# First attention layer of a four-layer network on one core: the order of statistics, norms and transposes between the value and key products of its prologue

## The chip, the core and the metric

The kernel runs on one core of one Trainium2 chip. A core has five engines that run side by side and wait for one another through semaphores: PE (TensorE, matrix products and transposes; its weight loads are listed as PEld), DVE (VectorE, elementwise work and row statistics), ACT (ScalarE, copies with a function), POOL (GpSimd) and SP (SyncE, which here issues the DMAs). Each engine works off its own instructions in the order in which the program lists them. What counts is the device time of one execution in microseconds (us), the median of several runs.

## The reference

Four layers on x of 2048 rows and 640 columns: attention, Fourier mixing, attention, Fourier mixing, each with a layer norm ahead of it and a residual sum behind it.

```python
def _A_ref(x, wqkv, wo):                     # attention, 32 heads of 20, window 256
    qkv = (x @ wqkv).reshape(B, S, 3, H, Dh) ...
    scores = einsum("bhqd,bhkd->bhqk", q, k) * Dh ** -0.5
    p = softmax(where(mask, scores, -1e9))
    return einsum("bhqk,bhkd->bhqd", p, v) ... @ wo
def _B_ref(x, Cr, Ci, Dr, Di):               # Fourier mixing, real part
    return Cr @ (x @ Dr.T) - Ci @ (x @ Di.T)
x = x + _A_ref(_layernorm(x), wqkv, wo)
x = x + _B_ref(_layernorm(x), ...)
x = x + _A_ref(_layernorm(x), wqkv, wo)
x = x + _B_ref(_layernorm(x), ...)
```

## The kernel before

The order of the work is written out by hand: nothing is moved by a scheduler, so each engine's queue is the order of the calls in the Python code. Every product is made of three products of halves: a value is cut in a high part (ACT, line 159) and a low part (the rest, a subtraction on DVE or POOL, line 165), and high times high, high times low and low times high are summed (`product3`, line 172).

The rows of x are handled as 16 tiles of 128 rows. In the first attention layer a tile t goes through these steps:

- `prep_load` (line 249): SP issues the load of 320 KB. Tiles 0 to 11 go to eight slots that are used in turn (tile t again in slot t modulo 8), tiles 12 to 15 to a ring of five buffers named x.
- `prep_stats` (lines 217 to 224): mean and variance on DVE (two statistics instructions, one that joins them, one that adds epsilon), then the power -0.5 on POOL (line 224).
- `prep_norm` (line 235): one DVE instruction, in place, which needs POOL's result.
- `prep_turn` (lines 260 to 275): five transposes on PE (line 272), four into one of the banks 2 and 3 (role x4) and the fifth into bank 4, the only one of role x1. Behind each group ACT takes the high part and DVE the low part out of the bank into `big`, the transposed x of 512 rows. So a turn has two ACT and two DVE instructions.

`before_heads` strings these together with the products that use them. `value(t)` makes the values of a tile in two halves of 15 matmuls each (lines 371 and 172, 128x320) and calls `prep()` between the two halves; the two results are copied out by ACT (line 394) and DVE (line 396) and every second tile is stored (line 398). `pieces(sb)` makes the first two of the ten chunks of queries and keys for 512 rows: `piece(c, sb, "q")` is 15 matmuls of 128x512, then the high and the low part of the result (tile c, lines 159 and 165) and its store (line 481). Behind each piece stands `split_w` and, in some cases, `prep()`.

`prep()` carries a counter r = `state[0]`, 2 at first. One call loads a later tile, takes the statistics of tile r+2, the norm of tile r+1 and the turn of tile r, in this order, and raises r. With the calls in the program's order, r is 2, 3, 4 in `value(1)` to `value(3)`, 5 and 6 in `pieces(0)`, 7 to 10 in `value(4)` to `value(7)`, 11 and 12 in `pieces(1)`, and 13 to 16 in `value(8)` to `value(11)`. Behind `pieces(0)`, `packed(0)` has SP fetch the stored queries and keys (line 535). `pieces(2)` and `pieces(3)` come when all tiles are turned; a call there finds no tile left.

`cut_chunk` (line 159 on ACT, line 165 on POOL for the first two chunks) cuts the weights of a chunk in high and low parts; it stands ahead of `value(1)` and of `value(2)`. The second attention layer enters `before_heads` with eight tiles ready (`first` is false), and the heads, the output product and the Fourier layers follow in both.

Of the kernel before, what the change touches and what calls it, by code (L numbers as in the profile page):

```python
# [63 lines left out]
class Net:  # L64
# [234 lines left out]
    def before_heads(self, xsrc):  # L299
        nc, a = self.nc, self.a  # L300
        self.proj = self.project()
        ready = self.ready
        first = ready == 0
# [8 lines left out]
        state = [2, 8] if first else [ready, ready + 4]  # L312
# [14 lines left out]
        else:  # L327
            self.prep_stats(ready + 1)

        def prep():  # L330
            r = state[0]
            if state[1] < r + (8 if first else 5):
                self.prep_load(xsrc, state[1])
                state[1] += 1
            self.prep_stats(r + 2)
            self.prep_norm(r + 1)
            self.prep_turn(r)
            state[0] += 1

        def split_w(n):  # L340
            for _ in range(n):
                if wl and next(wl[0], 1) is not None:
                    wl.pop(0)

        def pieces(sb):
            for c in range(2):
                self.piece(c, sb, "q")
                split_w(4)
                if ready or state[0] < 4 * sb + 9:
                    prep()  # L350

        def opening():
            self.prep_stats(0)
# [23 lines left out]
        def value(t):  # L377
            v, xt = vst[t // 2 % 2], self.xnt(t // 4)
            rs = slice((t % 4) * P, (t % 4 + 1) * P)
            ps = [self.bank("v", 320) for _ in range(2)]  # L380
            if t or not first:
                for hf, p in enumerate(ps):
                    cs = slice(hf * 320, (hf + 1) * 320)
                    self.all3(p, [((xt[:, 0, k, rs], xt[:, 1, k, rs]), (wv[k][0][:, cs], wv[k][1][:, cs]))
                                  for k in range(KC)])
                    if hf == (not first):
                        prep()
            else:
                first_value(ps)
            for hf in range(2):  # L390
                dst = v[:, 4 * hf:4 * hf + 4, t % 2, 0:84].rearrange("p q (h c) -> p q h c", c=21)[:, :, :, 1:21]
                src = ps[hf].rearrange("p (q h c) -> p q h c", q=4, h=4)
                if hf == 0:
                    nc.scalar.activation(dst, src, AF.Copy)
                else:
                    nc.vector.tensor_copy(dst, src)  # L396
            if t % 2:
                nc.sync.dma_start(self.vd[:, :, t - 1:t + 1, :].rearrange("q p t c -> p q (t c)"),
                                  v.rearrange("p q t c -> p q (t c)"))
# [12 lines left out]
        if first:  # L412
            opening()
            for t in range(4):
                if t in (1, 2):
                    self.cut_chunk(t - 1)
                value(t)
            nc.gpsimd.tensor_copy(self.mask, mask)
            pieces(0)
        else:  # L420
            pieces(0)
            pieces(1)
            values(0)
# [1331 lines left out]
```

## Time and profile before

| | us |
|---|---|
| median of 3 runs | 2169.33 |
| lowest and highest of them | 2168.49, 2171.95 |
| the profiled execution's own time | 2170.36 |
| span of its trace | 2168.6 |
| prologue of the first attention layer, ahead of its heads | 0 to about 122 |

The profile is one execution on the chip, seen by the hardware profiler. Its page gives the busy time of each engine; its timeline gives each engine's instructions in order of time, with adjacent ones of a kind merged: start, length, engine, line, operation, what is written from what is read, the count, and in brackets the time that the engine sat idle before it with the instruction that released it. The chain of waits follows the work that ended last back from the end. Instruction times are us unless marked ns. The span is shorter than the execution's own time by 1.76 us, which lie ahead of the first and behind the last instruction.

### The profile page before, as it was taken

The page shows a single profiled execution, that of the slowest core. Times are in us where ns is not written, and L with a number is a line of the kernel's source. Part 1 is how long each engine was busy: PE and PEld are TensorE (multiplying, and loading weights), DVE is VectorE, ACT ScalarE, POOL GpSimd, SP SyncE. Part 2 cuts the span into 40 slices and gives each one's busy share as a digit, 9 for nine tenths or more (in the row PEclk, how much of TensorE's full clock was granted, in tenths as well). Part 3 has the DMA queues.
Part 4 walks back from the last instruction along what each step waited for, and adds up shares of the span by engine and source line. Part 5 has one row for each costly group of instructions (what it writes and reads, how often), then busy time and mean ns, then how long its engine had stood idle before and what let it go on. Part 6 is the DMA issues. An engine that isn't in the chain of part 4 may idle for free.

```text
span 2168.6 us, 49267 instructions
## 1 busy us (share of the span) xinstructions
PE 2116.1 (98%) x17893; PEld 1766.9 (81%) x17893; DVE 1609.8 (74%) x3936; ACT 1167.4 (54%) x2611; POOL 921.7 (43%) x1455
## 2 busy tenths in 40 slices
PE   8999999899999999999999999998999999999999
PEld 7987777687878888889999877776877788888899
DVE  7348888686897868787751588887778868787777
ACT  2217877766554545543431288787765545455522
POOL 2037776776524233230130477778754323241300
PEclk9999999999999999999999999999999999999999
DMA  6446666786435453657646466667854354546653
GB/s 202 159 161 195 200 195 212 211 223 202 135 122 179 133 188 127 221 195 259 219 137 188 151 201 190 209 198 222 235 182 136 125 189 136 165 152 215 224 173 125
DMA packets 221619, 395.41 MB, mean 182 GB/s; under 512 B 39360, under 2 KB 85952, under 8 KB 221376
## 3 DMA queue, kind: packets, MB, share of 16 engines
q1 hardware_dynamic: 221376, 392.26, 57.3%
q8 instruction: 141, 2.31, 0.5%
q14 instruction: 102, 0.84, 0.1%
HBM read 273.94 MB, written 117.05 MB: 180 GB/s over the span
## 4 chain that ended last, share of the span: by engine, by line
PE 81%; DVE 7%; POOL 4%; ACT 4%; issue 2%; DMA 2%; SPq 0%; ACTq 0%; DVEq 0%; POOLq 0%
PE banks L1294 27%; PE banks L172 15%; PE banks L190 14%; PE banks L638 8%; PE banks L1549 6%; PE banks L608 6%; PE banks L578 4%; POOL ou L1224 1%; POOL big L165 1%; DVE qp L165 1%; ACT big L956 1%; PE banks L272 1%; DVE st L217 1%; PE banks L590 1%; POOL rs L1006 1%
## 5 line engine op out<-in xcount | busy, mean ns | idle before, releaser
L583 DVE CUSTOM_DVE_ANT_0 banks<-banks,mask 128x384 f32<-128x384 f32 (+2 forms) x1024 | 525.2, 558 | 154.6 <-PE banks L578 116.8
L617 ACT ACTIVATE pt<-banks 128x384 f32<-128x384 f32 (+2 forms) x1024 | 430.0, 472 | 140.6 <-PE banks L578 62.3
L608 PE MATMUL banks<-qp,kp 61*128 61x384 f32 (+2 forms) x1024 | 303.0, 365 | 10.8 <-DMA qp<-mt 8.8
L623 POOL TENSOR_SCALAR_AFFINE_SELECT pt<-pt 128x256 f32<-128x256 f32 x512 | 211.1, 413 | 179.5 <-ACT pt L617 130.2
L578 PE MATMUL banks<-kp,qp 60*128 60x384 f32 (+2 forms) x1024 | 279.7, 360 | 4.7 <-DVE mc L583 4.2
L190 PE MATMUL banks<-big,wc 64*128 64x512 f32 x1920 | 272.1, 394 | 0.4 <-DVE pt L396 0.4
L608 PEld LDWEIGHTS banks<-qp,kp 61*128 61x128 f32 x1024 | 176.8, 185 | 68.8 <-issue 28.3
L638 PE MATMUL banks<-pt,vq 128*32 128x128 f32 x5760 | 214.7, 278 | 3.7 <-POOL pt L623 3.7
L190 PEld LDWEIGHTS banks<-big,wc 64*128 64x128 f32 x1920 | 183.0, 185 | 29.4 <-ACT x L502 6.7
L638 PEld LDWEIGHTS banks<-pt,vq 128*32 128x32 f32 x5760 | 144.0, 109 | 64.0 <-issue 47.9
L578 PEld LDWEIGHTS banks<-kp,qp 60*128 60x128 f32 x1024 | 163.6, 185 | 27.7 <-DVE mc L583 16.6
L1224 POOL TENSOR_TENSOR pt<-pt,pt 128x512 f32<-128x512 f32 x36 | 61.0, 1693 | 293.5 <-DMA pt<-c 248.9
L627 POOL TENSOR_SCALAR_AFFINE_SELECT pt<-pt 128x256 f32<-128x256 f32 x448 | 185.0, 413 | 0.0
L159 ACT ACTIVATE c<-pt 128x512 fp32r<-128x512 f32 x150 | 93.5, 626 | 147.3 <-POOL pt L1200 52.2
L159 ACT ACTIVATE qp<-pt 128x512 fp32r<-128x512 f32 (+1 forms) x195 | 119.6, 624 | 86.5 <-DVE pt L1225 36.1
L165 DVE TENSOR_TENSOR c<-pt,c 128x512 fp32r<-128x512 f32 x150 | 123.9, 835 | 50.6 <-ACT c L159 48.4
L165 DVE TENSOR_TENSOR qp<-pt,qp 128x512 fp32r<-128x512 f32 (+1 forms) x195 | 151.8, 791 | 10.6 <-ACT qp L159 7.9
L1294 PE MATMUL banks<-qp,big 128*128 128x512 f32 x630 | 151.2, 391 | 4.8 <-DVE qp L165 3.9
L583 DVE DVE_READ_ACCUMULATOR2_ANT mc<- 128x1 f32 x1024 | 144.3, 141 | 0.0
L1294 PEld LDWEIGHTS banks<-qp,big 128*128 128x128 f32 x630 | 117.0, 188 | 30.9 <-DVE qp L165 5.5
L1294 PE MATMUL banks<-qp,xc 128*128 128x512 f32 x480 | 118.0, 391 | 1.9 <-DVE xc L165 1.4
L1294 PEld LDWEIGHTS banks<-qp,xc 128*128 128x128 f32 x480 | 89.8, 188 | 22.5 <-DVE xc L165 2.3
(227 smaller groups left out, 4374.1 us busy)
## 6 DMA issues: line engine op xcount, KB each, us to landing
pt<-c SPq DMA_DIRECT2D x188, 512.0 KB
qk_d<-c SPq DMA_DIRECT2D x80, 512.0 KB
kp<-qk_d SPq DMA_DIRECT2D x384, 80.0 KB
qp<-qk_d SPq DMA_DIRECT2D x384, 80.0 KB
kp<-u_d SPq DMA_DIRECT2D x32, 640.0 KB
o_d<-ou SPq DMA_DIRECT2D x64, 256.0 KB
x_d<-x SPq DMA_DIRECT2D x48, 320.0 KB
v_d<-pt SPq DMA_DIRECT2D x16, 768.0 KB
```

Of the source, the lines that this page charges most:

```text
L159: nc.scalar.activation(hi, src, AF.Copy, scale=-1.0 if neg else 1.0)
L165: (eng or nc.vector).tensor_tensor(out=lo, in0=src, in1=hi.bitcast(F32), op=OP.subtract)
L172: self.nc.tensor.matmul(p, x, y, start=n == 0, stop=n == last)
L190: self.nc.tensor.matmul(ps[a], x[r], y[r], start=half + i == 0, stop=half == 1 and i == n - 1, skip_group_check=True)
L578: nc.tensor.matmul(p, qp[quad % 2][b:b + 60, z, qb * P:(qb + 1) * P], kp[quad % 2][b:b + 60, z, k0 * P:(qb + 1) * P], start=True, stop=True)
L583: nc.vector.tensor_tensor_reduce(out=p, in0=p, in1=self.mask[:, 384 - n * P:], scale=1.0, scalar=NEG, op0=OP.add, op1=OP.max, accum_out=mc ...
L608: nc.tensor.matmul(self.banks[:, tb[e], :n * P], kp[quad % 2][b:b + 61, z, kb * P:(kb + 1) * P], qp[quad % 2][b:b + 61, z, kb * P:(kb + n) ...
L617: nc.scalar.activation(pt[quad, kb][:, 2 * z + e, :n * P], self.banks[:, tb[e], :n * P], AF.Exp, scale=SCALE)
L623: nc.gpsimd.affine_select(out=t[:, :, 0:P], in_=t[:, :, 0:P], pattern=[[0, 2], [1, P]], compare_op=OP.is_ge, fill=0.0, base=0, channel_mul ...
L627: nc.gpsimd.affine_select(out=t[:, :, 256:384], in_=t[:, :, 256:384], pattern=[[0, 2], [-1, P]], compare_op=OP.is_gt, fill=0.0, base=0, ch ...
L638: nc.tensor.matmul(p[32 * h:32 * h + 32, :], vq[:, 96 * (kb % 4) + 21 * h:96 * (kb % 4) + 21 * h + 32], t[:, h, (qb - kb) * P:(qb - kb + 1 ...
L1294: nc.tensor.matmul(self.banks[:, bk, :], p, b[q], start=start and m == 0, stop=stop and last and m == 2, skip_group_check=True)
```

## The change

Two things are reordered in `before_heads`, both for the first layer only. In the call of `prep()` with r = 2 (inside `value(1)`) the turn of tile 2 is listed ahead of the statistics of tile 4 and the norm of tile 3. In `pieces(0)` and `pieces(1)` the statistics and the norm that belonged to the `prep()` behind a piece are listed ahead of that piece; its load and its turn stay behind it. No instruction is added or taken away, and the second attention layer's order is the same as before.

```diff
-        def prep():
+        def prep(ahead=False):
             r = state[0]
             if state[1] < r + (8 if first else 5):
                 self.prep_load(xsrc, state[1])
                 state[1] += 1
-            self.prep_stats(r + 2)
-            self.prep_norm(r + 1)
-            self.prep_turn(r)
+            if first and r == 2:
+                self.prep_turn(r)
+            if not ahead:
+                self.prep_stats(r + 2)
+                self.prep_norm(r + 1)
+            if not first or r > 2:
+                self.prep_turn(r)
             state[0] += 1
...
         def pieces(sb):
             for c in range(2):
+                ahead = first and state[0] < 4 * sb + 9
+                if ahead:
+                    self.prep_stats(state[0] + 2)
+                    self.prep_norm(state[0] + 1)
                 self.piece(c, sb, "q")
                 split_w(4)
-                if ready or state[0] < 4 * sb + 9:
-                    prep()
+                if ready or ahead:
+                    prep(ahead)
```

## The prediction

> **What bounds the kernel now.** I read the page first, then the busy time by stretches, then PE's and DVE's timelines of the prologue side by side.
>
> ```profile
> PE 2116.1 (98%) x17893; PEld 1766.9 (81%) x17893; DVE 1609.8 (74%) x3936; ACT 1167.4 (54%) x2611; POOL 921.7 (43%) x1455
> ```
>
> ```profile
> 0.00:122.00 122.00, 111.82 (x682) 103.86 (x682) 61.43 (x146) 29.33 (x66) 16.86 (x24) 1.00 0.57 182
> ```
>
> PE is busy 98% of the span. Of the prologue (columns: PE, PEld, DVE, ACT, POOL, granted clock, DMA share, GB/s) it is busy 111.82 of 122 us, so 10.2 us are idle, at full clock. Between 19 and 80 us PE's list of waits holds three, the ones in brackets in the timelines below: 1.09 + 0.41 + 0.47 = 1.97 us. The rest of the idle time lies ahead of 19 or behind 80 us, where the change moves nothing. All three waits are for DVE, which is busy half of the prologue: its order, not its load, is late.
>
> **The change, part by part. Part A: the turn of tile 2.** PE, then DVE:
>
> ```profile
> 21.98 0.46 PE L172 MATMUL banks<-kp,big 128*128 128x320 f32 x2
> 23.53 1.29 PE L172 MATMUL banks<-kp,big 128*128 128x320 f32 x7 [1.09 <-DVE big L165]
> ...
> 25.53 0.71 PE L272 MATMUL banks<-ident,big 128*128 128x128 f32 x5
> 26.00 1.56 PE L172 MATMUL banks<-kp,big 128*128 128x320 f32 x9
> ...
> 28.28 1.48 PE L172 MATMUL banks<-kp,big 128*128 128x320 f32 x9
> ...
> 30.48 0.71 PE L272 MATMUL banks<-ident,big 128*128 128x128 f32 x5
> ```
>
> ```profile
> 20.26 0.48 DVE L396 COPY pt<-banks 128x320 f32<-128x320 f32 x1
> 20.66 0.88 DVE L217 BATCH_NORM_STATS2 st<-big 128x6 f32<-128x320 f32 x2
> ...
> 21.82 0.15 DVE L221 TENSOR_SCALAR rs<-mv 128x1 f32<-128x1 f32 x1
> 21.89 0.99 DVE L235 TENSOR_SCALAR big<-big,mv,rs 128x640 f32<-128x640 f32 x1
> 22.80 0.88 DVE L165 TENSOR_TENSOR big<-banks,big 128x512 fp32r<-128x512 f32 x2
> ```
>
> The value product of tile 2 starts at 21.98; its third matmul needs tile 2's low part, which DVE makes at 22.80, behind the statistics of tile 4 and the norm of tile 3. How much is lost is read from start to start: the undisturbed product runs from 28.28 to the transposes at 30.48, 2.20 us; the disturbed one from 21.98 to 25.53, 3.55. The loss is 1.35 us, not 1.09, since the queue of weight loads stops as well.
>
> After the change the low part follows the copy at 20.26 directly. ACT's high part was ready:
>
> ```profile
> 19.87 0.77 ACT L159 ACTIVATE big<-banks 128x512 fp32r<-128x512 f32 x2 [2.28 <-PE banks L272]
> ```
>
> So it lies at about 20.66 to 21.54, ahead of the product: 1.35 us come back. Late next is the norm of tile 3, for the turn at 25.53 - 1.35 = 24.18. Statistics from 21.47 to 22.77 (1.30, as before), norm 0.60 to 0.99: done between 23.4 and 23.8, so 0.4 to 0.8 us to spare. If that cover failed, at most the split's 0.88 would come back as a wait. PE, ACT and SP keep their order here. On POOL the power of tile 4 comes about 0.4 us later, and by as much the weight cut behind it:
>
> ```profile
> 23.25 1.57 POOL L165 TENSOR_TENSOR wc<-x,wc 128x640 fp32r<-128x640 f32 x1
> ```
>
> Its first user is the second piece, which starts at 37.12 (below), so that costs nothing.
>
> **Parts B and C: statistics and norms ahead of the pieces.** PE around `pieces(0)`, then DVE:
>
> ```profile
> 36.66 0.71 PE L272 MATMUL banks<-ident,big 128*128 128x128 f32 x5
> 37.12 3.66 PE L172 MATMUL banks<-big,wc 128*128 128x512 f32 x15
> 40.62 0.71 PE L272 MATMUL banks<-ident,big 128*128 128x128 f32 x5
> 41.09 1.56 PE L172 MATMUL banks<-kp,big 128*128 128x320 f32 x9
> ...
> 43.95 1.12 PE L272 MATMUL banks<-ident,big 128*128 128x128 f32 x5 [0.41 <-DVE big L235]
> 44.83 1.42 PE L172 MATMUL banks<-kp,big 128*128 128x320 f32 x8
> ```
>
> ```profile
> 33.42 0.49 DVE L396 COPY pt<-banks 128x320 f32<-128x320 f32 x1 [0.79 <-PE banks L172]
> 37.48 0.69 DVE L165 TENSOR_TENSOR c<-banks,c 128x512 fp32r<-128x512 f32 x1 [3.57 <-ACT c L159]
> 38.09 0.88 DVE L217 BATCH_NORM_STATS2 st<-big 128x6 f32<-128x320 f32 x2
> ...
> 39.84 0.88 DVE L165 TENSOR_TENSOR big<-banks,big 128x512 fp32r<-128x512 f32 x2
> 41.45 0.69 DVE L165 TENSOR_TENSOR c<-banks,c 128x512 fp32r<-128x512 f32 x1 [0.73 <-ACT c L159]
> 42.06 0.88 DVE L217 BATCH_NORM_STATS2 st<-big 128x6 f32<-128x320 f32 x2
> ...
> 43.28 0.60 DVE L235 TENSOR_SCALAR big<-big,mv,rs 128x640 f32<-128x640 f32 x1
> 43.80 0.88 DVE L165 TENSOR_TENSOR big<-banks,big 128x512 fp32r<-128x512 f32 x2
> ```
>
> Undisturbed, 15 matmuls behind a turn take 2.28 us (26.00 to 28.28) and a turn 0.47 (40.62 to 41.09). So the turn of tile 7 was due at 41.09 + 2.28 = 43.37 and the next matmul at 43.84; it came at 44.83. The loss is 0.99 us, in two steps: the transposes wait for the norm (43.28 + 0.60), and the fifth for bank 4, which tile 6's low part empties only at 43.80 + 0.88 = 44.68.
>
> Statistics and norm together hold DVE from 42.06 to 43.88, 1.82 us. In the new order the first pair falls into DVE's idle 3.57 us ahead of 37.48. The second follows tile 5's low part (now behind 38.17): 38.1 + 0.9 + 1.8 = 40.8, and the piece's low part at 41.45 waits for ACT anyway, so 0.65 us are to spare. Tile 6's low part is then done at 42.1 + 0.9 = 43.0, 0.4 us ahead of the turn due at 43.37, which asks for bank 4 last. All 0.99 come back. If the cover went (DVE 0.65 us later), the piece's split and bank 4 would slip by the excess alone.
>
> `pieces(1)` is the same with tile 13:
>
> ```profile
> 69.83 1.56 PE L172 MATMUL banks<-kp,big 128*128 128x320 f32 x9
> ...
> 72.75 1.13 PE L272 MATMUL banks<-ident,x 128*128 128x128 f32 x5 [0.47 <-DVE x L235]
> 73.63 1.13 PE L172 MATMUL banks<-kp,big 128*128 128x320 f32 x6
> ```
>
> Due at 69.83 + 2.28 + 0.47 = 72.58, came at 73.63: 1.05 us.
>
> **The wait that is added** is for loaded tiles: the statistics of tile 13 now stand ahead of the piece, at about 60.3: behind DVE's last copy there, 62.14 + 0.49, less the 2.34 of A and B. Behind them in DVE's queue wait the piece's split and the turn's, and behind these PE.
>
> ```profile
> 62.14 0.49 DVE L396 COPY pt<-banks 128x320 f32<-128x320 f32 x1 [0.79 <-PE banks L172]
> ```
>
> ```profile
> 50.24 0.84 SPq L249 DMA_DIRECT2D x<-x  x2
> ```
>
> ```profile
> 4.08 7.12 DMA big<-x
> ```
>
> Tile 13's load is issued at 50.24. The slowest tile load that the chain shows took 7.12 us, behind the first weights. That gives 57.4 at the latest: hidden, with 2.9 us to spare. Shorter landings leave more. No DMA is moved past another; the moved steps issue none.
>
> **The sum:** 1.35 + 0.99 + 1.05 = 3.39 us. If only the idle column came back it would be 1.97; I take 3.39, because starts show what the matmuls lost and the merged lengths overlap. The other bounds are 0 and 3.39 plus what a later wait gains (below).
>
> The Trainium skill (Perfetto Trace Analysis, "Identifying the Most-Contended Engine") says that busy matmul time is a poor measure of headroom, since pipelined instructions look smaller, and judges by weight-load time. By the idle time of matmuls the sum would be 1.97, by starts 3.39; this trace bears the rule out where 1.09 us of idle time stand against 1.35 lost.
>
> From the profiled execution's 2170.36 us that makes 2166.97; it lay 1.03 above the median of the runs shown, so the median goes from 2169.33 to 2165.9. What is behind 122 us is in the same order on all queues and is released by earlier work, so it moves forward as a whole.
>
> **Rivals.** 0.2% is 4.3 us, about what a measurement of this kernel can tell from no change.
>
> Only the idle time returns (1.97), or new waits of 0.4 at A, B and C eat 1.2: 2167.1 to 2167.4. For it: the spare times are 0.4 to 0.8 us. Against: each is worked out from measured starts.
>
> The norm of tile 4 meets POOL's cut. For it: in the row at 21.89 a norm took 0.99, not 0.60, beside POOL's cut; against: the turn of tile 3 waits for ACT behind it. Price 0.39 at most, 2166.3; chance 0.05. The Trainium skill (GPSIMD Engine Reference, "1. Specifications") says that POOL's SBUF interfaces are shared with DVE's two-port instructions; the row at 21.89 fits it.
>
> Later waits for DMA move. These rows are the largest of PE's waits behind the prologue:
>
> ```profile
> PE banks L608 <- DMA qp<-mt: 8.8, 2, 5.3
> ```
>
> ```profile
> L594 SPq DMA_DIRECT2D qp<-mt x128: 504/538/949, 143.2 to 1572.1; - x128
> ```
>
> Of 128 such transfers (row maxima, for the heads) two hold PE, for 5.3 and 8.8 - 5.3 = 3.5 us. Their landing depends on what other transfers are on their way. If the earlier prologue frees one or both: 2165.9 - 3.5 = 2162.4, or 2157.1.
>
> **The other side:** a third transfer of row maxima is caught. One costs 5.3: 2171.2, slower than before by 0.09%. It decides against the change from 3.4 us of added waiting, and beyond 0.2% from two (2176.5). For it: 126 of them are so far hidden. Against: their issues shift along with what they compete with.
>
> The change doesn't do what it says: DVE is held elsewhere, no gain, 2169.3. Against it stand the idle rows above.
>
> **How the numbers follow.** Forecast 0.52 (own range 2164.4 to 2167, some run spread in it); small gain 0.09, the meeting on POOL 0.05; freed DMA waits 0.11; no gain 0.09; caught DMA 0.14. Faster by over 0.2% means under 2165.0: the freed waits, and with a spread of the runs of 1.7 us a third of the forecast, 0.11 + 0.18 = 0.29. Slower by over 0.2% (above 2173.7): half of the caught, 0.07. The range 2162.4 to 2171.2 leaves out the two ends, under 2 in 10.
>
> **What would show it.** PE's first product of the heads stands here:
>
> ```profile
> 121.51 0.33 PE L578 MATMUL banks<-kp,qp 60*128 60x128 f32 x2
> ```
>
> It should come at about 118.1, with PE's three waits gone; DVE's low part of tile 2 directly behind the copy; transposes of tiles 7 and 13 0.47 us long in place of 0.88. Wrong: a DVE wait for an x load ahead of a piece, a new PE gap at tile 3's turn, or a different time of the two waits for row maxima.

## The result and the profile after

The changed kernel takes 2166.71 us (median of 21 runs, 2164.8 to 2169.47); the kernel before took 2170.59 on the same chips (21 runs, 2168.4 to 2172.49). The ratio is 0.9982, 95% interval 0.9977 to 0.9988: 3.9 us less. The profiled execution's own time is 2166.44, its span 2164.7, against 2170.36 and 2168.6.

The line numbers behind `before_heads` are 8 higher in the changed kernel (line 404 is 396 before, 586 is 578). First the prologue as one stretch of its profile (columns as in the prediction: PE, PEld, DVE, ACT, POOL, granted clock, DMA share, GB/s), then PE's timeline at the three places.

```profile
0.00:118.10 118.10, 109.79 (x682) 103.20 (x682) 60.96 (x146) 29.34 (x66) 16.94 (x24) 1.00 0.58 188
```

```profile
16.38 1.48 PE L172 MATMUL banks<-kp,big 128*128 128x320 f32 x9
...
21.58 1.48 PE L172 MATMUL banks<-kp,big 128*128 128x320 f32 x9
...
23.78 0.71 PE L272 MATMUL banks<-ident,big 128*128 128x128 f32 x5
...
39.35 1.56 PE L172 MATMUL banks<-kp,big 128*128 128x320 f32 x9
...
41.63 0.71 PE L272 MATMUL banks<-ident,big 128*128 128x128 f32 x5
42.09 1.56 PE L172 MATMUL banks<-kp,big 128*128 128x320 f32 x9
...
67.09 1.56 PE L172 MATMUL banks<-kp,big 128*128 128x320 f32 x9
...
69.83 1.56 PE L172 MATMUL banks<-kp,big 128*128 128x320 f32 x9
...
117.69 0.33 PE L586 MATMUL banks<-kp,qp 60*128 60x128 f32 x2
```

All three waits, which stood in brackets before, are gone. From the start of tile 2's product to the next transposes it now takes 23.78 - 21.58 = 2.20 us where it took 3.55 (1.35 less). From the product of tile 4 to the next behind tile 7's turn it is 42.09 - 39.35 = 2.74 in place of 44.83 - 41.09 = 3.74 (1.00 less), and at tile 13 69.83 - 67.09 = 2.74 in place of 3.80 (1.06 less): 3.41 in all. In the columns of the stretch about half of the 3.9 us is idle PE time: 122 - 111.82 = 10.2 us before, 118.1 - 109.79 = 8.3 after. The other 2.0 had been booked as busy PE time, 0.85 of it in the start-up ahead of tile 1's products (9.05 us busy there before, 8.20 after), which the change doesn't touch.

A yardstick for what follows: the time from the first value product of tile 1 to the first product of the heads. It was 121.51 - 16.76 = 104.75 before (16.76 is the same product's start there) and is 117.69 - 16.38 = 101.31, 3.44 less. The other 0.38 of the 3.82 by which the heads start earlier lies ahead of it, in the start-up. Behind the heads' first product the two spans have 2047.09 and 2047.01 us left: in these two executions the gain is carried to the end. That they agree so closely is luck. In the eight profiles below that leave everything behind the prologue as it is, the rest takes between 2045.1 and 2051.1 us, so only the medians of many runs speak of whole executions.

The same stretch, before and after:

```profile
16.76:121.51 104.75, 102.45 (x643) 95.66 (x641) 49.09 (x122) 23.05 (x56) 15.02 (x18) 1.00 0.52 163
16.38:117.69 101.31, 101.26 (x642) 95.70 (x640) 48.79 (x122) 23.05 (x56) 15.11 (x18) 1.00 0.53 170
```

PE's idle time falls from 2.30 to 0.05 us, by 2.25 of the 3.44. That of its weight loads (second busy time) falls from 9.09 to 5.61, by 3.48: there nearly the whole gain stands as idle time. These are the waits of the weight loads at the three places in the kernel before:

```profile
23.53 1.02 PEld L172 LDWEIGHTS banks<-kp,big 128*128 128x128 f32 x7 [1.35 <-DVE big L165]
43.94 0.42 PEld L272 LDWEIGHTS banks<-ident,big 128*128 128x128 f32 x4 [0.67 <-DVE big L235]
44.74 0.14 PEld L272 LDWEIGHTS banks<-ident,big 128*128 128x128 f32 x1 [0.38 <-DVE big L165]
72.74 0.42 PEld L272 LDWEIGHTS banks<-ident,x 128*128 128x128 f32 x4 [0.73 <-DVE x L235]
73.54 0.14 PEld L272 LDWEIGHTS banks<-ident,x 128*128 128x128 f32 x1 [0.38 <-DVE big L165]
```

They add up to 3.51 us, and they show the two steps of the second and third loss apart: the norm holds the first four transposes, bank 4 the fifth. None of the five is left in the changed kernel.

DVE of the changed kernel, at the turn of tile 2 and around `pieces(0)`:

```profile
19.87 0.48 DVE L404 COPY pt<-banks 128x320 f32<-128x320 f32 x1
20.27 0.88 DVE L165 TENSOR_TENSOR big<-banks,big 128x512 fp32r<-128x512 f32 x2
...
22.29 0.60 DVE L235 TENSOR_SCALAR big<-big,mv,rs 128x640 f32<-128x640 f32 x1
...
24.44 0.76 DVE L235 TENSOR_SCALAR big<-big,mv,rs 128x640 f32<-128x640 f32 x1
...
32.08 0.88 DVE L217 BATCH_NORM_STATS2 st<-big 128x6 f32<-128x320 f32 x2
...
35.73 0.69 DVE L165 TENSOR_TENSOR c<-banks,c 128x512 fp32r<-128x512 f32 x1 [1.82 <-ACT c L159]
...
39.72 0.69 DVE L165 TENSOR_TENSOR c<-banks,c 128x512 fp32r<-128x512 f32 x1 [0.76 <-ACT c L159]
40.33 0.88 DVE L165 TENSOR_TENSOR big<-banks,big 128x512 fp32r<-128x512 f32 x2
```

The low part of tile 2 (the row at 20.27) stands directly behind the copy. The idle slot ahead of the first piece's split has shrunk from 3.57 to 1.82 us: the first pair sits in it. Ahead of the second split 0.76 are still idle, so DVE is on time, and tile 6's low part ends at 41.21, 0.42 ahead of the turn at 41.63. The statistics of tile 13 started without a wait for their load:

```profile
59.40 0.49 DVE L404 COPY pt<-banks 128x320 f32<-128x320 f32 x1 [0.78 <-PE banks L172]
59.81 0.88 DVE L217 BATCH_NORM_STATS2 st<-x 128x6 f32<-128x320 f32 x2
```

### The profile page after: what moved, and what is told of

Read it like the earlier page. It is cut to its first block, busy times and chain, and to the rows that moved or that the text cites. A ratio compares the mean times of both kernels' runs of the same rounds, so it can differ in the third digit from the quotient of the medians.

```text
span 2164.7 us, 49267 instructions
## 1 busy us (share of the span) xinstructions
PE 2114.2 (98%) x17893; PEld 1766.6 (82%) x17893; DVE 1611.1 (74%) x3936; ACT 1167.2 (54%) x2611; POOL 920.8 (43%) x1455
## 4 chain that ended last, share of the span: by engine, by line
PE 84%; DVE 6%; POOL 4%; ACT 4%; DMA 2%; issue 1%; ACTq 0%; POOLq 0%; DVEq 0%; SPq 0%
PE banks L1302 29%; PE banks L172 15%; PE banks L190 14%; PE banks L646 8%; PE banks L1557 6%; PE banks L616 6%; PE banks L586 4%; POOL big L165 1%; PE banks L272 1%; ACT big L964 1%; DVE qp L165 1%; POOL ou L1232 1%; PE banks L598 1%; POOL rs L1014 1%; DVE st L217 1%
```

## The experiments

### Each part alone

Three kernels have one part of the change each. Part A alone leaves the pieces in the old order; the other two kernels have the old `prep()` order and move the pair for one `sb` only.

```diff
-                ahead = first and state[0] < 4 * sb + 9
+                ahead = False                                               # part A alone
+                ahead = first and sb == 0 and state[0] < 4 * sb + 9         # first pieces alone
+                ahead = first and sb == 1 and state[0] < 4 * sb + 9         # second pieces alone
...
-                if ready or ahead:
+                if ready or state[0] < 4 * sb + 9:
```

> Part A alone: tile 2's turn ahead, the pieces in the old order. Measured on PE from the first value product of tile 1 to the first product of the heads: 104.75 us before, 101.31 with the whole change. Theory (the three losses add up, A is worth 1.35): 103.40, with 0.4 to 0.5 us of idle time left at the turns of tiles 7 and 13, and a span about 1.3 under the one before. Rival (one common lateness of DVE, which a part alone only shifts to the next place): 104.2 or more, with larger gaps at tiles 7 and 13.

> Statistics and norms ahead of the pieces in the first 512 rows only, all else in the old order. Theory: 104.75 - 1.00 = 103.75 on the same stretch, PE idle by 1.09 ahead of tile 2's product and by 0.47 at tile 13's turn, no gap at tile 7's. Rival (common lateness): the gap at tile 13 grows by about 1 and the stretch stays at 104.75.

> The same for the second 512 rows only. Theory: 104.75 - 1.05 = 103.70, with PE's gaps of 1.09 and 0.41 unchanged. Rival (the gain at a late place is eaten behind it): no gap at tile 13, but new PE gaps between tile 13's turn and the heads, 104.5 or more. All three parts together should make 3.40.

Measured on the yardstick: 103.39 for part A, 103.71 for the first pieces, and 102.40 for the second, 1.3 less than the theory had for it. All of PE's waits from 17 to 122 us in the first kernel (part A alone), then in the second (the first pieces alone):

```profile
PE banks L272 <- DVE x L235: 0.5, 1, 0.5
PE banks L272 <- DVE big L235: 0.4, 1, 0.4
PE banks L190 <- DVE pt L404: 0.4, 1, 0.4
```

```profile
PE banks L172 <- DVE big L165: 1.1, 1, 1.1
PE banks L272 <- DVE x L235: 0.5, 1, 0.5
PE banks L190 <- DVE pt L401: 0.4, 1, 0.4
```

In each the part's own wait is gone and the others stand at their old size. The last line of both is the wait at the entry of the heads, which was there before. The third kernel's profile had an odd start:

```profile
14.56 1.33 PE L272 MATMUL banks<-ident,big 128*128 128x128 f32 x5 [0.62 <-DVE big L235]
15.54 3.28 PE L376 MATMUL banks<-qp,big 128*128 128x320 f32 x12
18.65 1.48 PE L172 MATMUL banks<-kp,big 128*128 128x320 f32 x9
```

Twelve matmuls took 3.28 us that take 2.00 elsewhere. PE came to tile 1's product 1.9 us later, DVE had caught up by then, and part A's wait had shrunk. So the kernel was profiled once more:

> The same kernel as in the run of the second pieces alone, whose profile had PE's first products slow until 18.65 us and a stretch of 102.40. Theory (the slow start gave DVE time and hid part A's wait there): with a start near 16.4 to 16.9 the gap of 1.09 ahead of tile 2's product is back and the stretch is 103.7. Rival (part A's gap goes away when the second pieces are reordered): 102.4 again with an ordinary start.

```profile
16.98 1.48 PE L172 MATMUL banks<-kp,big 128*128 128x320 f32 x9
...
23.74 1.29 PE L172 MATMUL banks<-kp,big 128*128 128x320 f32 x7 [1.08 <-DVE big L165]
```

With an ordinary start the gap of 1.08 is back, and the yardstick is 103.68. The parts are then worth 104.75 - 103.39 = 1.36, 1.04 and 1.07: 3.47 against 3.44 for all together. They add up, and the rival of one common lateness, which a part alone would only shift to the next place, falls.

The times of whole executions can't show this. Against the kernel before the ratios are 0.9995 (0.9985 to 1.0004), 0.9997 (0.9988 to 1.0007) and 1.0001 (0.9992 to 1.001): each interval holds both no change and the 0.05 to 0.06% that a part is worth on the yardstick. That a single part's gain reaches the end is not shown.

### What the pieces' order hangs on

One kernel moves the pair (statistics and norm) only ahead of the second piece; the first piece's pair stays behind it. Another keeps all of it behind the piece but puts the turn first, so that bank 4 is emptied early and the norm comes late.

```diff
-                ahead = first and state[0] < 4 * sb + 9
+                ahead = first and c == 1 and state[0] < 4 * sb + 9          # second pair alone
...
-                if ready or ahead:
+                if ready or state[0] < 4 * sb + 9:
```

```diff
-        def prep(ahead=False):
+        def prep(early=False):                                              # turn first
...
-            if first and r == 2:
+            if first and r == 2 or early:
                 self.prep_turn(r)
-            if not ahead:
-                self.prep_stats(r + 2)
-                self.prep_norm(r + 1)
-            if not first or r > 2:
+            self.prep_stats(r + 2)
+            self.prep_norm(r + 1)
+            if not first or r > 2 and not early:
                 self.prep_turn(r)
...
-                ahead = first and state[0] < 4 * sb + 9
-                if ahead:
-                    self.prep_stats(state[0] + 2)
-                    self.prep_norm(state[0] + 1)
+                early = first and state[0] < 4 * sb + 9
...
-                if ready or ahead:
-                    prep(ahead)
+                if ready or early:
+                    prep(early)
```

> The whole change, but the pair that belongs to the first piece of each 512 rows stays behind that piece; only the second piece's pair is moved ahead. Theory (the slot ahead of the second piece's split holds some 0.7 us more than the pair of that piece): DVE runs about 0.9 late at the second piece's split, tile 6's low part ends near 42.1 and bank 4 comes 0.1 to 0.4 late; the stretch is 101.5 to 102.0. Rival (the whole loss hangs on the norm of tiles 7 and 13 alone): 101.3, no gap. Rival (both pairs must move): 102.7 or more.

> Part A as in the change; in the pieces the turn is put ahead of statistics and norm, but all of them stay behind the piece. So bank 4 is emptied as early as in the change, and the norm of tiles 7 and 13 comes later than before. Theory (the turn waits for its norm first): norm of tile 7 ends near 42.95 where the turn is due at 41.6, 1.36 lost at each of the two places, stretch from tile 1's product to the heads 101.31 + 2.7 = 104.0. Rival (the wait is one for bank 4): 101.3.

Measured: 101.66 and 104.28. PE at tile 7's turn with the second pair alone:

```profile
41.71 0.86 PE L272 MATMUL banks<-ident,big 128*128 128x128 f32 x5
42.33 1.57 PE L172 MATMUL banks<-kp,big 128*128 128x320 f32 x9
```

and with the turn first:

```profile
43.51 0.76 PE L272 MATMUL banks<-ident,big 128*128 128x128 f32 x5 [1.05 <-DVE big L235]
44.03 1.56 PE L172 MATMUL banks<-kp,big 128*128 128x320 f32 x9
```

In the first the transposes start on time and only the fifth waits: 0.62 us from the turn to the next matmul in place of 0.46, twice, which is most of the 0.35. In the second the transposes wait 1.05 us for the norm and then run through without a wait for bank 4. From the product ahead of the turn to the product behind it the second kernel loses 1.27 us at tile 7 and 1.30 at tile 13, near the 1.36 expected; most of the other 0.4 is lost at the turns of tiles 6 and 12, 0.18 each. So each of the two releases that the prediction named can hold PE by itself. In the kernel before, the norm weighed more: 0.67 and 0.73 us of the weight loads' waits, against 0.38 for bank 4.

### How much cover DVE has

Here one and two instructions without use (a memset of 1.34 us) are put on DVE ahead of the second piece of the first 512 rows.

```diff
+                for _ in range(1 if ahead and c == 1 and sb == 0 else 0):   # 2 in the second kernel
+                    nc.vector.memset(self.pt[2], 1.0)
                 self.piece(c, sb, "q")
```

> The whole change, with one DVE memset of 128x1536 (1.34 us) added ahead of the second piece of the first 512 rows, behind the norm of tile 7. Theory (0.7 us of cover at that split and some 0.8 more at bank 4): the split slips by 0.6, tile 6's low part ends at about 41.8, in front of bank 4's use at 42.0: nothing lost, stretch 101.3. Rival (no cover, DVE sets the pace there): 101.9.

> Two such memsets (2.68 us). Theory: the split slips by 1.9, bank 4 is emptied at 43.1, the next matmul starts 1.1 to 1.4 late: stretch 102.4 to 102.7. Rival (the piece's split and bank 4 hold nothing up, the norm alone does): 101.3.

Measured: 101.32 with one filler, 102.97 with two. With one, DVE's split of the second piece slips, and nothing else moves:

```profile
39.23 1.34 DVE L356 MEMSET pt<- 128x1536 f32 x1 [0.27 <-issue]
40.48 0.63 DVE L165 TENSOR_TENSOR c<-banks,c 128x512 fp32r<-128x512 f32 x1
41.02 0.88 DVE L165 TENSOR_TENSOR big<-banks,big 128x512 fp32r<-128x512 f32 x2
```

The low part of tile 6 now ends at 41.90 in place of 41.21, and PE doesn't notice: bank 4 is used last by the turn at 41.63. With two, PE's timeline shows the wait for that bank by itself:

```profile
41.77 0.60 PE L272 MATMUL banks<-ident,big 128*128 128x128 f32 x4
43.81 0.33 PE L272 MATMUL banks<-ident,big 128*128 128x128 f32 x1 [1.45 <-DVE big L165]
```

Four transposes on time, the fifth 1.45 us late. The 1.65 lost are more than the 1.1 to 1.4 expected because the two fillers held DVE for more than their 2.68 us: from the norm's end at 39.08 to the piece's split at 42.34 it was 3.26, with a gap ahead of each (0.27 and 0.39 us). So the cover at this place is real: tile 6's low part can come 0.69 us later at no cost, and DVE becomes the bound somewhere between one filler and two.

### The largest waits left

The prediction's rivals hung on PE's waits for transfers of row maxima (qp<-mt): the scores' maxima of four heads (a quad), which the heads' second score product on line 616 needs. In the changed kernel these waits stand at 8.7 us:

```profile
PE banks L616 <- DMA qp<-mt: 8.7, 2, 4.7
```

They are for the same two transfers, of quad 6 (counted from 0), second block of 512 rows, once in each attention layer. The first of three kernels has ACT issue them; the other two are meant to put them further forward on SP.

```diff
-                self.post(1, lambda z=z: nc.sync.dma_start(
+                self.post(1, lambda z=z: (nc.scalar if (quad, u) == (6, 1) else nc.sync).dma_start(
```

> The whole change, and the two transfers of row maxima of quad 6, second block, in each attention layer are issued by ACT's queue, not by SP's. In the trace of the changed kernel ACT had these maxima at 410.2 and SP issued them only at 414.75, and PE waited 4.0 and 4.7 us for them. Theory (these waits are SP's queue, not the chip's DMA load): both vanish, the time falls by 6 to 9 us to about 2159. Rival (the landing is late because the DMA engines are full, or the wait moves on to the next transfer): less than 2 us.

2183.67 us, ratio 1.0058 (1.0045 to 1.0072): slower than the kernel before. ACT and SP in that profile:

```profile
404.52 8.20 SPq L792 DMA_DIRECT2D x<-o_d  x2
...
410.48 1.68 ACTq L602 DMA_DIRECT2D qp<-mt  x2
412.26 0.97 ACT L625 ACTIVATE pt<-banks 128x128 f32<-128x128 f32 x4 [1.81 <-PE banks L586]
```

SP's wait and, 30 us later, PE's:

```profile
SPq L792 <- DMA qp<-mt: 7.1, 1, 7.1
442.25 0.65 PE L616 MATMUL banks<-qp,kp 61*128 61x384 f32 x1 [4.51 <-DMA qp<-mt]
```

The two issues held ACT for 1.68 us. And on SP the second of a pair of loads, issued in 1.62 us together in the changed kernel, waited 7.1 us, by the profile for these very transfers: it stands ahead of them in the program and is issued from another queue, and still it was issued only at 412.2, when the first of them had moved its data (at about 411.8). Why a load waits for a later transfer is open. PE no longer waits for these two transfers, but the next maxima hold it for 4.51 us here and 4.20 in the other attention layer, 8.7 in all as before, and its waits for POOL in the heads (line 646) rise from 4.0 to 9.2 us. The rest of the 17.0 us by which this kernel is slower than the changed one isn't accounted for. So the wait moved on to the next transfer, as the rival had it, but neither foresaw the cost; with ACT and SP both held, the run doesn't tell what the place in SP's queue is worth.

```diff
+            put = (lambda f: f()) if (quad, u) == (6, 1) else (lambda f: self.post(1, f))
...
-                self.post(1, lambda z=z: nc.sync.dma_start(
+                put(lambda z=z: nc.sync.dma_start(
...
+            if rows != (6, 1):
                 for f in later.pop(step, []):
                     f()
...
                         m_rows(*rows)
+                        for f in later.pop(step, []):
+                            f()
```

> The whole change, and in both attention layers the two transfers of row maxima of quad 6, second block, stand on SP ahead of the three key loads and the one store that preceded them (some 1.05 + 0.39 us of issue, and what SP waited for there); ACT issues nothing. Theory (PE's waits of 4.0 and 4.7 us come from the place in SP's queue): the transfers are issued 1.5 to 2 us earlier, each wait shrinks by as much, the time falls by 3 to 4 us below the changed kernel's, to about 2163. Rival (the transfer lands late because of what is on its way, or the next maxima inherit the wait): within 1 us of the changed kernel.

2166.59 us, ratio 0.9986 (0.9977 to 0.9995), and SP issued the transfers at 414.88: three key loads of the same step were issued through a second call and still stood ahead. So the transfers were issued no earlier, and the theory wasn't tested. The last kernel holds these loads back too:

> As in the run before this one, but with the key loads that are issued at once also put behind: now the two transfers of row maxima of quad 6, second block, stand ahead of one x load and three key loads (in the last run these still stood ahead of them, and SP issued them at 414.88 as before). Theory (PE's waits of 4.0 and 4.7 us come from the place in SP's queue): issued at 411 to 412, each wait shrinks by 2 to 4 us, the time falls by 4 to 8 us below the changed kernel's, to about 2161. Rival (the next maxima, or the loads put behind, inherit the wait): within 2 us of the changed kernel.

2167.71 us, ratio 0.9988 (0.9979 to 0.9997). SP and then PE in its profile:

```profile
412.18 1.46 SPq L603 DMA_DIRECT2D qp<-mt  x2
```

```profile
417.36 0.43 PE L617 MATMUL banks<-qp,kp 61*128 61x384 f32 x1 [0.89 <-ACT pt L626]
432.82 0.41 PE L617 MATMUL banks<-qp,kp 61*128 61x384 f32 x1 [2.41 <-DMA qp<-mt]
```

The transfers are issued 2.6 us earlier than in the changed kernel, and PE's wait of 4.0 at this place is gone. In its stead the next maxima are late, by 2.41 us (2.58 in the other attention layer). In all, PE waits 5.0 us for maxima instead of 8.7, and 2.5 instead of 0.3 for ACT's exponentials (line 626). No gain shows in the times: the median is 1.0 us above the changed kernel's, with runs from 2163.78 to 2170.05. None of the three versions is measurably faster than the changed kernel.

## Why the prediction was right

- **The three losses.** Put at 1.35, 0.99 and 1.05; 1.35, 1.00 and 1.06 in the trace, and 1.36, 1.04 and 1.07 alone. Starts were the right thing to read: PE's three listed waits had 1.97, its idle time over the stretch 2.25. The reason given for the first, that the queue of weight loads stops as well, is borne out: the weight loads waited 1.35 us there.
- **Part A's next wait.** The norm of tile 3 ends at 22.29 + 0.60 = 22.89, 0.89 us ahead of its turn at 23.78; 0.4 to 0.8 were forecast. It met no POOL cut.
- **The meeting on POOL.** It was given a chance of 0.05 and it came: tile 4's norm (24.44, 0.76 us) ran beside POOL's cut, which lasted from 23.27 to 24.84. It cost PE nothing, though not for the reason given: tile 3's low part followed the norm at once (25.12) instead of waiting for ACT, and ended at 25.99, ahead of its product at 26.53. The Trainium skill (GPSIMD Engine Reference, "1. Specifications") names the shared SBUF interfaces; 0.76 beside a cut against 0.60 without agrees, at less than half the price that was set on it.
- **The pieces.** 0.65 to spare at the second split, 0.76 measured; 0.4 at bank 4, 0.42 measured to the start of the turn. The real cover there is larger, since the fifth transpose comes last: with one filler the low part ended at 41.90, 0.27 behind the turn's start, and PE lost nothing. With a second one it did.
- **The added load wait.** Hidden, as said: the statistics of tile 13, put at about 60.3, started at 59.81 directly behind the copy.
- **The heads' first product.** 118.1 forecast, 117.69 measured. The 0.4 are the start-up, which the sum didn't hold.
- **The time.** 2165.9 forecast from a median of 2169.33 of three runs, 2166.71 measured. Over 21 runs the kernel before has 2170.59, so the forecast started 1.26 too low and the gain came out 0.5 larger; that the two partly cancel is luck. The forecast gain was 3.4; the measured one is 3.9 between the medians, whose interval, 2.6 to 5.0 us, doesn't tell them apart. At 0.18% it lies inside the 0.2% that stood for no measurable change; with 21 runs a side it could be told from none.
- **The other side.** The same two transfers of row maxima held PE, for 8.7 us in all where it was 8.8 (5.3 and 3.5 in the two layers became 4.0 and 4.7). No third one was caught and none freed.

What stays open is whether each part alone carries its whole gain to the end of an execution.

## What to carry to other kernels

When the bound engine waits for an engine that is far from full, look for work that stands ahead of the late result and isn't needed yet, and for an idle slot of the same queue to move it into; price the move by start-to-start distances of the bound engine against an undisturbed neighbour. PE's listed waits held only 1.97 of the 3.41 us lost here, those of its weight loads 3.51. Then name what is late next and by how much it is covered. And a wait taken away in one place of a long queue of transfers may only pass to the next one.

## What the runs showed of the hardware that was not expected

The same first products ran at different speeds in different executions while the granted clock read 1.00 throughout. The first 18 value matmuls took 5.36 us in the kernel before and 4.50 in the changed one:

```profile
8.58 5.36 PE L371 MATMUL banks<-kp,big 128*128 128x320 f32 x18 [0.47 <-ACT big L159]
```

```profile
8.58 4.50 PE L379 MATMUL banks<-kp,big 128*128 128x320 f32 x18 [0.47 <-ACT big L159]
```

In one run (the second pieces alone) the slow stretch lasted until 18.6 us, and the granted clock, the third column from the right, is 1.00 there too:

```profile
14.60:18.60 4.00, 4.00 (x17) 4.00 (x18) 2.68 (x7) 1.04 (x3) 0.07 (x1) 1.00 0.80 307
```

That shifted the prologue by up to 1.9 us and hid most of part A's wait, so part A's worth depends on it. The Trainium skill (TensorE: Matmul & The Clock Gate, "What's actually happening") says that TensorE starts at half clock until a window of activity has passed and that the window doesn't start with the kernel, so the point of change differs from run to run; the different lengths agree with that. The half microsecond either way that the page gives for the point of change is less than here, where the speed changed within the first 18 matmuls, which end at 13.08, in one run and at about 18.6 us in another. The granted clock of the profile doesn't show it.

A norm on DVE that started beside a weight cut on POOL ended at a fixed distance behind the cut. Alone a norm takes 0.60 us. In the kernel before it overlapped the cut's last 0.63 us and ended at 22.88, 0.36 behind the cut's end at 22.52; in the changed kernel it overlapped the last 0.40 and ended at 25.20, again 0.36 behind the end at 24.84. In all 13 profiles the distance is 0.34 to 0.36. So in these runs the price of such a meeting is the time of overlap less 0.24 us: 0.39 and 0.16 here.

With two transfers issued from ACT's queue, a load on SP that stands ahead of them waited 7.1 us, by the profile until the first of them had landed, and the two issues took 1.68 us of ACT's time.
